# Banded attention and two gated blocks: softmax weights turned in one VectorE instruction per pair and moved by on-chip DMAs

## The chip, the cores and the metric

The kernel runs on one core of one Trainium2 chip. The metric is the device time of one execution in microseconds, the median of three runs. Engines are named as in the profile: PE is TensorE (matrix products; PEld its weight loads), DVE is VectorE, ACT is ScalarE, POOL is GpSimd, SP is SyncE, whose queue issues the DMAs here.

## What is computed

Eight batches of 576 tokens go through an attention of eight heads of width 64 and two gated blocks of width 512. Each query sees at most 32 keys: itself and the 31 before it in heads 0 to 3, every fourth of the 128 positions up to itself in heads 4 to 7.

```python
def _attn_ref(q, k, v):
    scores = scale * np.matmul(q, k.transpose(0, 1, 3, 2))
    mask_plain = (rel >= 0) & (rel < window)                       # window 32
    mask_dil = (rel >= 0) & (rel < window * dilation) & (rel % dilation == 0)   # dilation 4
    scores = np.where(masks[None, :, :, :], scores, -1000000000.0)
    scores = scores - np.max(scores, axis=-1, keepdims=True)
    attn = np.exp(scores)
    attn = attn / (np.sum(attn, axis=-1, keepdims=True) + 1e-09)
    return np.matmul(attn, v)

def _moe_ref(x, w_val, conv_w, w_out):        # gate: causal convolution over 5 tokens
    gate = 1.0 / (1.0 + np.exp(-gate_pre))
    return (gate * (x @ w_val)) @ w_out

def _moe2_ref(x, w_in, w_spatial, b_spatial, w_out):
    h = np.maximum(x @ w_in, 0.0)             # u and v are its halves
    v_n = (v - mu) / np.sqrt(var + 1e-06)
    v_s = np.einsum('ts,bsd->btd', w_spatial, v_n) + b_spatial[None, :, None]
    return (u * v_s) @ w_out
```

## The kernel before

**Attention.** A batch is worked on in four pairs of heads. The 576 queries of a head form 18 blocks of 32, and a block sees 64 keys in a row (tokens of the dilated heads are ordered by their remainder by four first). The score tile of a pair, s_ps, has 128 partitions and nine slots of 64 keys. Partition quarter 2e + h holds block BLOCK[e][x] of head h in slot x. For batch 0 `a_scores` (L287) makes 36 products, each with 64 rows of keys and queries of one head and 32 query columns. For the other batches (L281) it makes 18 of full height, in which the queries of the two heads stand apart with zeros beside them. PE works on each product of float32 in two passes, so a pair leaves 72 or 36 records in the trace. `a_max` (L300 to L307), `a_exp` (ACT) and `a_sum` (L329 to L333, the last of them on POOL) make the weights e_t, a tile of one buffer.

**Turning the weights.** The product with the values needs keys on partitions. The tile pt holds the weights turned, in a form of 128 partitions (keys) by six groups of three blocks. Its zeros are written once, with batch 0, whose weights PE turns. For the other batches `a_trans` issues 16 DVE transposes per pair (L367), one for each partition quarter, half of the 64 keys and run of slots that goes to one place in pt: eight of 32 by 192 elements, eight of 32 by 96. `a_pv` (L384) multiplies six groups for two heads, 12 products into o_ps, which ACT copies to xt (L389, L391). `a_split` makes xh on ACT and xl = xt − xh on POOL; `a_conv` (L417, L419) makes the gate's convolution with five DVE instructions; `a_tanh` ends it on ACT.

**The gated blocks.** A batch is 37 steps: eight val steps (12 products each from xh, xl and the split weight), five v, eight u, eight sp and eight out. A step's products share one of four PSUM buffers of the pool ps_m. val is emptied by DVE (L459), u by ACT, sp by DVE's vb and ru (L546, L547), then split by ACT (g2h) and POOL (g2l), out by ACT (ob), which SP stores (L560). Products of split weights count three for one: high by high, high by low, low by high.

**What sets the order.** The steps of batch b are events 0 to 36. Attention of batch b + 1 is put among them by a table, pair p at 8 p plus an offset: scores 0, max 1, exp 3, sum 3.6, transposes 9, pv 10, split 11, conv 11.2, tanh 12.5. Pair 3's transposes so stand at 33, among the eight out steps (29 to 36). Batch 0's attention is ordered by hand (PRELUDE), and the making of the weights from float64 is placed in batch 0 by a table (FIRST). A scheduler then orders each engine's instructions by its own estimate of when they can run, so the order on an engine is not that of the code.

**Buffers.** s_ps and o_ps have one buffer each; qk, vv, xt and most short-lived tiles have two. The loads of the pair two further on are issued in `a_scores` and `a_pv`, as soon as the old tile has been read.

Of the kernel before, what the change touches and what calls it, by code (L numbers as in the profile page):

```python
# [8 lines left out]
F32 = mybir.dt.float32  # L9
# [20 lines left out]
QZ = KEYS + 2 * S  # the same with the queries of the two heads set apart by zeros  # L30

# Queries come in 18 blocks of 32. Partition half e, slot x of a score tile holds block BLOCK[e][x] of
# both heads. Block 3 j + i sees keys 32 i to 32 i + 63 of group j. RUNS are slots with one i each.
# [7 lines left out]
# Upper words of the float64 that float32's range begins and ends with, read as float32.  # L41
# [3 lines left out]
# What is issued before the first batch's matrix products, in order, and what goes in between them,  # L45
# with its place among them.
# [105 lines left out]
def attention_gated_mlp_kernel(  # L152
    ctx: ExitStack,
    tc: tile.TileContext,
    qk0: bass.AP,
# [23 lines left out]
    pt = const.tile([128, NJ, 3, 2, QB], F32, name="pt")  # L179
# [11 lines left out]
    def weight(name):  # L191
        # A weight whose memory serves something else until the weight is made.
        if name not in held:
            held[name] = wts.tile(LATE[name], F32R, tag=name, name=name)
        return held[name]
# [5 lines left out]
    def split(raw, hi, lo):  # L201
        # raw = hi + lo exactly, where hi has the bits that one pass carries.
        nc.scalar.copy(out=hi, in_=raw)  # L203
        nc.gpsimd.tensor_tensor(out=lo, in0=raw, in1=_f(hi), op=ALU.subtract)  # L204
# [17 lines left out]
    # ---- attention: one batch and one pair of heads at a time  # L222
# [14 lines left out]
    def load_qk(b, p):  # L237
        b, p = b + p // NP, p % NP
        if b == B:
            return  # L240
        if b == 0 and p >= 2:
            t = early_tile(p)
        else:
            t = rot.tile([128, QZ], F32, tag="qk", name="qk_t")
        if b == 0:
            nc.sync.dma_start(out=t[:, 0:QC], in_=qk0[p])
        else:
            nc.sync.dma_start(out=t, in_=qk[b - 1, p])
        qk_t[b, p] = t
# [21 lines left out]
    def a_scores(b, p):  # L271
        t = qk_t.pop((b, p))
        s = ps_s.tile([128, 1024], F32, tag="s", name="s_ps")
        for i in range(2 * NS):
            x, e = divmod(i, 2)
            n = BLOCK[e][x]
            cols = slice(SW * x, SW * x + SW)
            keys = slice(QB * n, QB * n + SW)
            if b:
                q = t[:, KEYS + 64 * i:KEYS + 64 * i + 64]  # L280
                nc.tensor.matmul(s[64 * e:64 * e + 64, cols], q, t[:, keys], start=True, stop=True)  # L281
                continue
            for h in range(2):
                r = slice(64 * h, 64 * h + 64)
                q = t[r, KEYS + QB * n:KEYS + QB * n + QB]
                o = 64 * e + QB * h
                nc.tensor.matmul(s[o:o + QB, cols], q, t[r, keys], start=True, stop=True)  # L287
        if b or p >= 2:
            load_qk(b, p + 2)
        s_t[b, p] = s  # L290
# [44 lines left out]
    def a_trans(b, p):  # L335
        # The weights of the values, with keys on the partitions. TensorE turns the first batch's and
        # writes the zeros as well, which stay; VectorE turns the others'.
        e = e_t.pop((b, p))
        if b == 0:
# [10 lines left out]
            for g in range(3):  # L350
                ps = ps_m.tile([128, 512], F32, tag="m", name="t_ps")
                for i in range(3):
                    nc.tensor.transpose(ps[:, chunk(i)], padded[:, 3 * g + i, :], ident_sb)
                for q in range(2):
                    j, i = divmod(BLOCK[q][3 * g], 3)
                    nc.scalar.copy(
                        out=pt[:, j:j + 3, i],
                        in_=ps[:, 0:384].rearrange("p (j e h q) -> p e j h q", j=3, e=2, h=2)[:, q],
                    )
            return  # L360
        for q, lo, hi in RUNS:
            j, i = divmod(BLOCK[q][lo], 3)
            for h in range(2):
                r = 32 * (2 * q + h)
                for c in range(2):
                    k = 32 * (i + c)
                    nc.vector.transpose(  # L367
                        out=pt[k:k + 32, j:j + hi - lo, i, h], in_=e[r:r + 32, lo:hi, 32 * c:32 * c + 32]
                    )

    def a_pv(b, p):
# [8 lines left out]
        for j in range(NJ):  # L380
            c = 512 * (j // 3) + 96 * (j % 3)
            for h in range(2):
                r = slice(64 * h, 64 * h + 64)
                nc.tensor.matmul(o[r, c:c + 96], u[:, j, r], pt[:, j, :, h], start=True, stop=True)  # L384
# [38 lines left out]
    def a_tanh(b, p):  # L423
        # sigmoid(g) = (1 + tanh(g / 2)) / 2, the half of which goes into w2.
# [4 lines left out]
        (0, a_scores), (1, a_max), (3, a_exp), (3.6, a_sum), (9, a_trans),  # L429
# [6 lines left out]
    # ---- the two gated blocks: one batch, in steps of one accumulation each  # L436

    def mlp_steps(b):
# [29 lines left out]
        def vstep(i):  # L468
# [11 lines left out]
            else:  # L480
                # The last 64 tokens: the two parts of g sit side by side and are added afterwards.
# [18 lines left out]
        def vnorm(i):  # L500
# [7 lines left out]
            if i == 4:  # L508
                # The last 64 tokens a second time, of which the rest stays.
# [58 lines left out]
    # ---- weights: from float64 to float32, the two linear maps in a row made one, and split  # L568
# [25 lines left out]
    def from64(dst, src):  # L594
        # Sign and top bit of the exponent, its low bits and 20 of the mantissa from the upper word
        # (kept inside float32's range), three of the mantissa from the lower word.
# [58 lines left out]
    def fuse(key, e):  # L655
        # w2 = moe_w_out @ moe2_w_in / 2, one chunk of rows and one half of the columns.
# [17 lines left out]
    # ---- everything in order  # L674
# [28 lines left out]
def _layout(q, k, v, moe_w_val, moe_conv_w, moe_w_out, moe2_w_in, moe2_w_spatial, moe2_b_spatial, moe2_w_out):  # L703
# [3 lines left out]
    # The dilated heads see every fourth token: with tokens ordered by their remainder they see a  # L707
    # window like the others.
# [8 lines left out]
    order = np.array(BLOCK).T.reshape(-1)  # L717
    qk0 = np.zeros((NP, 2, D, QC), q.dtype)
    qk = np.zeros((B - 1, NP, 2, D, QZ), q.dtype)
    vv = np.zeros((B, NP, 128, NJ, 2, D), v.dtype)  # L720
    for p in range(NP):
        for hh in range(2):
            h = 2 * p + hh
            qt, kt = qp[:, h].transpose(0, 2, 1), kp[:, h].transpose(0, 2, 1)
            qk0[p, hh, :, 32:KEYS] = kt[0]
            qk0[p, hh, :, KEYS:] = qt[0]
            apart = np.zeros((B - 1, D, 2 * NS, 2, QB), q.dtype)
            apart[:, :, :, hh, :] = qt[1:].reshape(B - 1, D, 2 * NS, QB)[:, :, order]
            qk[:, p, hh, :, 32:KEYS] = kt[1:]
            qk[:, p, hh, :, KEYS:] = apart.reshape(B - 1, D, 2 * S)  # L730
# [8 lines left out]
    def words(w):  # L739
# [17 lines left out]
        ("qk0", qk0.reshape(NP, 128, -1)),  # L757
        ("qk", qk.reshape(B - 1, NP, 128, -1)),
# [32 lines left out]
```

## Time and profile before

| | us |
|---|---|
| median of three runs | 737.53 (736.53, 737.77, 737.53) |
| the profiled execution, as its span | 735.2 |
| left between that span and the median | 2.3 |
| PE busy | 681.2 (93%) |
| DVE busy | 605.4 (82%) |
| POOL, ACT busy | 319.9 (44%), 279.9 (38%) |

The profiled execution is a run of its own; the profile gives its time as the span from the first to the last instruction, and what lies around that span is in the median. The busy shares are means over stages that differ. In the first 180 us the weights are converted, multiplied together and split beside batch 0. Six stretches of 82 us follow, each with the blocks of one batch and the attention of the next. The last batch has no attention beside it. A stretch is delimited here by where val of a batch begins: 504.47 and 586.72 us for one.

### The profile page before, as it was taken

The numbers are of one execution on the slowest core, as the hardware profiler recorded it, in microseconds if no ns is written. First come the engines' busy times: TensorE is split into PE (matmuls) and PEld (weight loads), VectorE is DVE, ScalarE is ACT, GpSimd is POOL, SyncE is SP. The second block draws the span as 40 slices with busy tenths as digits, with TensorE's granted clock in tenths as the row PEclk, the third lists the DMA queues.
The fourth block names the chain that finished last, engine by engine and source line by source line (L and its number), as shares of the span: only waits on it lengthen the run. The fifth ranks groups of instructions, "written<-read, shape, count | busy, mean of one in ns | idle before, by whom it ended". The sixth has DMA issues, their size and how long they took to land.

```text
span 735.2 us, 14508 instructions
## 1 busy us (share of the span) xinstructions
PE 681.2 (93%) x5796; PEld 610.1 (83%) x5796; DVE 605.4 (82%) x1233; ACT 279.9 (38%) x603; POOL 319.9 (44%) x362
## 2 busy tenths in 40 slices
PE   3797999879999899989999899989998999989998
PEld 3455688768899798989899798979898898979898
DVE  5999889999699789996899789997899789984430
ACT  4664435224343324334343334333343334233422
POOL 2527945442644244344544254344534254344421
PEclk9998999989999999999999999999999999999999
DMA  8951023314022221313222221213222220001001
GB/s 345 403 190 49 2 79 120 126 52 136 22 71 72 87 77 53 106 53 112 71 72 81 79 97 48 98 46 112 72 72 80 85 93 22 24 25 42 1 1 64
DMA packets 22179, 63.24 MB, mean 86 GB/s; under 512 B 2528, under 2 KB 11104, under 8 KB 21600
## 3 DMA queue, kind: packets, MB, share of 16 engines
q1 hardware_dynamic: 22112, 62.32, 24.3%
q8 instruction: 45, 0.74, 0.4%
q14 instruction: 22, 0.18, 0.1%
HBM read 52.88 MB, written 9.44 MB: 85 GB/s over the span
## 4 chain that ended last, share of the span: by engine, by line
DVE 46%; PE 38%; issue 8%; ACT 4%; POOL 3%; DMA 1%; SPq 0%; ACTq 0%; DVEq 0%; POOLq 0%
DVE pt L367 14%; PE val_ps L208 12%; PE v_ps L208 8%; DVE tt L419 8%; PE out_ps L208 7%; DVE ru L547 3%; DVE vb L546 3%; PE u_ps L208 3%; PE w_ps L208 3%; PE sp_ps L208 2%; DVE v_t L502 2%; DVE st L490 2%; PE o_ps L384 2%; DVE sm L329 2%; PE s_ps L281 2%
## 5 line engine op out<-in xcount | busy, mean ns | idle before, releaser
L367 DVE STREAM_TRANSPOSE pt<-e_t 32x96 f32<-32x96 f32 (+1 forms) x448 | 143.1, 319 | 9.2 <-PE o_ps L384 1.4
L419 DVE SCALAR_TENSOR_TENSOR tt<-xt,cw,tt 128x576 f32<-128x576 f32 x128 | 134.1, 1049 | 2.2
L208 PE MATMUL sp_ps<-wsp_h,vh 128*128 128x288 f32 x320 | 94.9, 301 | 5.9 <-DVE vb L546 4.9
L204 POOL TENSOR_TENSOR g2l<-ru,g2h 128x288 fp32r<-128x288 f32 x64 | 58.8, 931 | 88.2 <-ACT g2h L203 83.7
L208 PE MATMUL out_ps<-g2h,wout_h 128*128 128x288 f32 x256 | 80.2, 314 | 18.3 <-DVE vb L546 11.8
L208 PE MATMUL sp_ps<-wsp_l,vh 128*128 128x288 f32 x320 | 93.5, 298 | 3.0 <-POOL wsp_l L204 3.0
L208 PE MATMUL out_ps<-g2l,wout_h 128*128 128x288 f32 x256 | 77.6, 304 | 0.0
L208 PE MATMUL u_ps<-gh,w_h 128*128 128x288 f32 x256 | 77.1, 301 | 0.0
L208 PE MATMUL sp_ps<-wsp_h,vl 128*128 128x288 f32 x256 | 76.0, 297 | 0.0
L208 PE MATMUL out_ps<-g2h,wout_l 128*128 128x288 f32 x256 | 75.9, 300 | 0.0
L208 PE MATMUL u_ps<-gh,w_l 128*128 128x288 f32 x256 | 75.5, 295 | 0.0
L208 PE MATMUL u_ps<-gl,w_h 128*128 128x288 f32 x256 | 75.5, 295 | 0.0
L204 POOL TENSOR_TENSOR gl<-tt,gh 128x288 fp32r<-128x288 f32 x64 | 53.3, 839 | 47.3 <-ACT gh L203 47.1
L208 PEld LDWEIGHTS out_ps<-g2h,wout_h 128*128 128x128 f32 x256 | 49.1, 192 | 24.7 <-DVE vb L546 15.3
L514 POOL TENSOR_TENSOR vl<-v_t,vh 128x512 fp32r<-128x512 f32 x32 | 42.0, 1315 | 57.6 <-ACT vh L506 57.6
L208 PEld LDWEIGHTS sp_ps<-wsp_h,vh 128*128 128x128 f32 x320 | 60.5, 189 | 7.8 <-DVE vb L546 5.7
L208 PE MATMUL val_ps<-xh,wval_h 128*128 128x288 f32 x224 | 66.6, 298 | 0.2
L208 PE MATMUL val_ps<-xl,wval_h 128*128 128x288 f32 x224 | 66.4, 296 | 0.0
L208 PE MATMUL val_ps<-xh,wval_l 128*128 128x288 f32 x224 | 66.0, 295 | 0.0
L426 ACT ACTIVATE tt<-tt 128x576 f32<-128x576 f32 x32 | 22.0, 686 | 109.5 <-DVE tt L419 105.5
L208 PEld LDWEIGHTS sp_ps<-wsp_l,vh 128*128 128x128 f32 x320 | 60.6, 190 | 3.1 <-POOL wsp_l L204 3.1
L208 PE MATMUL v_ps<-w_h,gh 128*128 128x512 f32 x160 | 60.9, 405 | 0.0
(129 smaller groups left out, 1688.3 us busy)
## 6 DMA issues: line engine op xcount, KB each, us to landing
qk_t<-in_qk SPq DMA_DIRECT2D x28, 880.0 KB, 4.5
vv_t<-in_vv SPq DMA_DIRECT2D x30, 384.0 KB, 3.1
out<-ob SPq DMA_DIRECT2D x64, 144.0 KB, 1.8
raw<-in_w_in SPq DMA_DIRECT2D x4, 1024.0 KB, 9.1
raw<-in_w_mid_t SPq DMA_DIRECT2D x2, 1024.0 KB, 9.7
raw<-in_w_val SPq DMA_DIRECT2D x2, 1024.0 KB, 13.5
raw<-in_w_out SPq DMA_DIRECT2D x4, 512.0 KB, 4.5
sp_raw<-in_w_sp_t SPq DMA_DIRECT2D x5, 288.0 KB, 2.9
```

Source lines behind the costliest of these rows:

```text
L204: nc.gpsimd.tensor_tensor(out=lo, in0=raw, in1=_f(hi), op=ALU.subtract)
L208: nc.tensor.matmul(o, a, r, start=(i == 0), stop=(i == len(pairs) - 1))
L281: nc.tensor.matmul(s[64 * e:64 * e + 64, cols], q, t[:, keys], start=True, stop=True)
L329: nc.vector.tensor_reduce(out=sm[:, :, 0], in_=e, axis=AX.X, op=ALU.add)
L367: nc.vector.transpose(out=pt[k:k + 32, j:j + hi - lo, i, h], in_=e[r:r + 32, lo:hi, 32 * c:32 * c + 32])
L384: nc.tensor.matmul(o[r, c:c + 96], u[:, j, r], pt[:, j, :, h], start=True, stop=True)
L419: nc.vector.scalar_tensor_tensor(out=t, in0=xt[:, k:k + S], scalar=cw[:, p, k:k + 1], in1=t, op0=ALU.mult, op1=ALU.add)
L426: nc.scalar.activation(out=t, in_=t, func=ACTF.Tanh, scale=0.5)
L490: nc.vector.bn_stats(out=st, in_=v)
L514: nc.gpsimd.tensor_tensor(out=low["v"][:, i], in0=v, in1=_f(h), op=ALU.subtract)
L546: nc.vector.tensor_tensor(out=tmp, in0=ps[:, 0:HS], in1=bb[:, h], op=ALU.add)
L547: nc.vector.tensor_tensor(out=r, in0=tmp, in1=r, op=ALU.mult)
```

## The change

`a_trans` for batches 1 to 7 turns the whole weight tile with one DVE transpose, 32 by 32 inside each partition quarter, into a new tile et of one buffer. Sixteen DMAs from SP's queue then carry its pieces to pt: eight of 32 partitions by 192 elements, eight by 96, in runs of 768 and 384 bytes. pt is laid out anew so that each piece is one run per partition. The offset of `a_trans` in the table goes from 9 to 6. `a_scores` uses the products of batch 0 for all batches, 36 per pair with 32 query columns each; the queries are loaded without zeros, 592 KB per pair for 880, and the separate input qk0 goes. In all, 448 transposes become 28, with 448 more DMAs of together 8.3 MB, and the loads shrink by about 8 MB.

```diff
-    pt = const.tile([128, NJ, 3, 2, QB], F32, name="pt")
+    pt = const.tile([128, 3, 2, NJ, QB], F32, name="pt")
...
-            t = rot.tile([128, QZ], F32, tag="qk", name="qk_t")
-        if b == 0:
-            nc.sync.dma_start(out=t[:, 0:QC], in_=qk0[p])
-        else:
-            nc.sync.dma_start(out=t, in_=qk[b - 1, p])
+            t = rot.tile([128, QC], F32, tag="qk", name="qk_t")
+        nc.sync.dma_start(out=t[:, 0:QC], in_=qk[b, p])
...
-            if b:
-                q = t[:, KEYS + 64 * i:KEYS + 64 * i + 64]
-                nc.tensor.matmul(s[64 * e:64 * e + 64, cols], q, t[:, keys], start=True, stop=True)
-                continue
             for h in range(2):
                 r = slice(64 * h, 64 * h + 64)
                 q = t[r, KEYS + QB * n:KEYS + QB * n + QB]
...
+        t = act.tile([128, 2, NS, QB], F32, tag="et", name="et")
+        nc.vector.transpose(
+            out=t.rearrange("p c x q -> p x c q"), in_=e.rearrange("p x (c k) -> p x c k", c=2)
+        )
         for q, lo, hi in RUNS:
             j, i = divmod(BLOCK[q][lo], 3)
-            for h in range(2):
-                r = 32 * (2 * q + h)
-                for c in range(2):
-                    k = 32 * (i + c)
-                    nc.vector.transpose(
-                        out=pt[k:k + 32, j:j + hi - lo, i, h], in_=e[r:r + 32, lo:hi, 32 * c:32 * c + 32]
-                    )
+            for c in range(2):
+                k = 32 * (i + c)
+                for h in range(2):
+                    r = 64 * q + 32 * h
+                    nc.sync.dma_start(out=pt[k:k + 32, i, h, j:j + hi - lo], in_=t[r:r + 32, c, lo:hi])
...
-                nc.tensor.matmul(o[r, c:c + 96], u[:, j, r], pt[:, j, :, h], start=True, stop=True)
+                nc.tensor.matmul(o[r, c:c + 96], u[:, j, r], pt[:, :, h, j], start=True, stop=True)
...
-        (0, a_scores), (1, a_max), (3, a_exp), (3.6, a_sum), (9, a_trans),
+        (0, a_scores), (1, a_max), (3, a_exp), (3.6, a_sum), (6, a_trans),
```

The order on DVE in a steady batch, where the sp steps end and the out steps begin. vb and ru empty a sp step, the tt rows are the convolution of pair 2, the transposes those of pair 3. Before:

```order
L417 TENSOR_SCALAR tt<-xt,cw 128x576
L419 SCALAR_TENSOR_TENSOR tt<-xt,cw,tt 128x576
L367 STREAM_TRANSPOSE pt<-e_t 32x6x32 x4
L367 STREAM_TRANSPOSE pt<-e_t 32x3x32
L546 TENSOR_TENSOR vb<-sp_ps,bb 128x288
L367 STREAM_TRANSPOSE pt<-e_t 32x3x32 x4
L419 SCALAR_TENSOR_TENSOR tt<-xt,cw,tt 128x576
L367 STREAM_TRANSPOSE pt<-e_t 32x3x32 x3
L367 STREAM_TRANSPOSE pt<-e_t 32x6x32 x4
L546 TENSOR_TENSOR vb<-sp_ps,bb 128x288
L547 TENSOR_TENSOR ru<-vb,ru 128x288
L419 SCALAR_TENSOR_TENSOR tt<-xt,cw,tt 128x576
```

After, lines moved by a few (L354 is the transpose, L540 vb, L541 ru, L413 the convolution):

```order
L322 RECIPROCAL sm<-sm 128x9
L354 STREAM_TRANSPOSE et<-e_t 128x9x2x32
L411 TENSOR_SCALAR tt<-xt,cw 128x576
L540 TENSOR_TENSOR vb<-sp_ps,bb 128x288
L413 SCALAR_TENSOR_TENSOR tt<-xt,cw,tt 128x576
L541 TENSOR_TENSOR ru<-vb,ru 128x288
L540 TENSOR_TENSOR vb<-sp_ps,bb 128x288
L413 SCALAR_TENSOR_TENSOR tt<-xt,cw,tt 128x576
L541 TENSOR_TENSOR ru<-vb,ru 128x288
L413 SCALAR_TENSOR_TENSOR tt<-xt,cw,tt 128x576 x2
```

The sixteen transposes, which stood in three pieces around two vb, are one instruction ahead of them.

The order on PE, where the out steps of a batch end. o_ps rows are the pv products of pair 3. Before, among the last out steps:

```order
L208 MATMUL out_ps<-g2h,wout_h 128x288
L384 MATMUL o_ps<-pt,vv_t 64x96 x2
L208 MATMUL out_ps<-g2l,wout_h 128x288
L208 MATMUL out_ps<-g2h,wout_l 128x288
L208 MATMUL out_ps<-g2l,wout_h 128x288
L208 MATMUL out_ps<-g2h,wout_l 128x288
L384 MATMUL o_ps<-pt,vv_t 64x96 x9
L208 MATMUL out_ps<-g2h,wout_h 128x288
```

After, with the last out product first; s_ps is pair 0 of the batch after:

```order
L206 MATMUL out_ps<-g2l,wout_h 128x288
L206 MATMUL out_ps<-g2h,wout_l 128x288
L278 MATMUL s_ps<-qk_t 32x64 x5
L378 MATMUL o_ps<-pt,vv_t 64x96
L278 MATMUL s_ps<-qk_t 32x64 x3
L378 MATMUL o_ps<-pt,vv_t 64x96 x11
L206 MATMUL val_ps<-xh,wval_h 128x288
```

The pv products of pair 3 have gone from among the out products to behind the last of them, with val of the next batch right after.

The val products that follow them, each tile with its number: 6009 and 6065 are the first two val steps, xh_5981 is the part of x that pair 3's pv makes.

```order
L206 MATMUL val_ps_6009<-xh_5797,wval_h_798 128x288
L206 MATMUL val_ps_6009<-xl_5314,wval_h_798 128x288
L206 MATMUL val_ps_6009<-xh_5797,wval_l_799 128x288
L278 MATMUL s_ps_6025<-qk_t_5475 32x64 x28
L206 MATMUL val_ps_6065<-xh_5313,wval_h_798 128x288
L206 MATMUL val_ps_6065<-xl_5314,wval_h_798 128x288
L206 MATMUL val_ps_6065<-xh_5313,wval_l_799 128x288
L206 MATMUL val_ps_6065<-xh_5542,wval_h_798 128x288
L206 MATMUL val_ps_6009<-xh_5981,wval_h_798 128x288
```

The product that needs the newest part of x stands behind the scores and four products of the second val step.

The order on SP in a steady batch, around the stores of the out steps (L560). Before:

```order
L560 DMA out<-ob 128x288 x6
L259 DMA vv_t<-in_vv 128x768
L560 DMA out<-ob 128x288 x2
L248 DMA qk_t<-in_qk 128x1760 x2
L259 DMA vv_t<-in_vv 128x768 x2
L560 DMA out<-ob 128x288 x16
```

After (L554 the stores, L363 the DMAs to pt, L243 and L254 the loads):

```order
L254 DMA vv_t<-in_vv 128x768
L363 DMA pt<-et 32x192 x4
L363 DMA pt<-et 32x96
L554 DMA out<-ob 128x288
L363 DMA pt<-et 32x96 x2
L554 DMA out<-ob 128x288
L363 DMA pt<-et 32x96 x5
L363 DMA pt<-et 32x192 x4
L554 DMA out<-ob 128x288 x4
L254 DMA vv_t<-in_vv 128x768
L554 DMA out<-ob 128x288 x2
L243 DMA qk_t<-in_qk 128x1184
```

Between two stores there are now up to nine of the sixteen DMAs to pt of pair 3.

## Rows read from the trace of the kernel before

**Rows 1.** The page's busy shares, and its chain of waits by engine.
```profile
PE 681.2 (93%) x5796; PEld 610.1 (83%) x5796; DVE 605.4 (82%) x1233; ACT 279.9 (38%) x603; POOL 319.9 (44%) x362
...
DVE 46%; PE 38%; issue 8%; ACT 4%; POOL 3%; DMA 1%; SPq 0%; ACTq 0%; DVEq 0%; POOLq 0%
```

**Rows 2.** Windows, one period: us, busy (x instructions) by engine, PEclk, DMA share, GB/s.
```profile
504.47:586.72 82.25, 79.17 (x698) 72.69 (x697) 72.08 (x156) 29.73 (x59) 34.74 (x41) 1.00 0.24 79
```

**Rows 3.** Waits of the whole run: engine, line, waited for: us in total, times, longest.
```profile
PE out_ps L208 <- DVE vb L546: 11.8, 12, 1.3
PE sp_ps L208 <- DVE vb L546: 4.9, 6, 0.9
...
PE out_ps L208 <- ACT wout_h L203: 4.6, 1, 4.6
...
PE sp_ps L208 <- POOL wsp_l L204: 3.0, 1, 3.0
...
PE out_ps L208 <- ACT g2h L203: 1.8, 6, 0.3
```

**Rows 4.** PE's timeline: start us, us, instruction, count [idle before <-releaser].
```profile
556.49 0.40 PE L208 MATMUL sp_ps<-wsp_h,vh 128*128 128x288 f32 x1 [0.80 <-DVE vb L546]
...
569.97 0.40 PE L208 MATMUL out_ps<-g2h,wout_h 128*128 128x288 f32 x1 [1.31 <-DVE vb L546]
...
583.43 0.30 PE L208 MATMUL val_ps<-xh,wval_h 128*128 128x288 f32 x1
583.56 0.29 PE L208 MATMUL val_ps<-xl,wval_h 128*128 128x288 f32 x1
```

**Rows 5.** DVE's timeline at the same boundary of the same batch.
```profile
567.65 1.78 DVE L367 STREAM_TRANSPOSE pt<-e_t 32x192 f32<-32x192 f32 x5
569.46 0.46 DVE L546 TENSOR_TENSOR vb<-sp_ps,bb 128x288 f32<-128x288 f32 x1
...
587.32 0.75 DVE L300 TENSOR_TENSOR e_t<-s_ps,mask_sb 128x576 f32<-128x576 f32 x1
```

**Rows 6.** Groups by line and shape: count | busy, mean ns of one | idle before.
```profile
L419 DVE SCALAR_TENSOR_TENSOR tt<-xt,cw,tt 128x576 f32<-128x576 f32 x128 | 134.1, 1049 | 2.2
...
L367 DVE STREAM_TRANSPOSE pt<-e_t 32x192 f32<-32x192 f32 x224 | 82.6, 369 | 4.4 <-POOL e_t L333 1.3
...
L367 DVE STREAM_TRANSPOSE pt<-e_t 32x96 f32<-32x96 f32 x224 | 60.5, 270 | 4.8 <-PE o_ps L384 1.4
```

**Rows 7.** PE's timeline: scores of the first batch, then of a later one.
```profile
11.00 2.14 PE L287 MATMUL s_ps<-qk_t 64*32 64x64 f32 x72 [3.31 <-DVE mx L302]
...
18.62 0.90 PE L353 MATMUL t_ps<-ident_sb,boot 128*128 128x128 f32 x3 [1.69 <-POOL boot L344]
...
26.63 1.21 PE L287 MATMUL s_ps<-qkv 64*32 64x64 f32 x72
27.77 1.20 PE L353 MATMUL t_ps<-ident_sb,boot 128*128 128x128 f32 x9
...
600.78 1.27 PE L281 MATMUL s_ps<-qk_t 128*64 128x64 f32 x36
```

**Rows 8.** SyncE's queue at the start, two issues one behind the other.
```profile
1.18 0.42 SPq L263 DMA_DIRECT2D mask_sb<-in_masks  x1
1.64 0.42 SPq L246 DMA_DIRECT2D qk_t<-in_qk  x1
```

**Rows 9.** The page's DMA issues: count, size, median us from issue to landing.
```profile
out<-ob SPq DMA_DIRECT2D x64, 144.0 KB, 1.8
```

**Rows 10.** A semaphore wait on PE's weight queue, min/median/max ns, in 540 to 543 us.
```profile
L384 PEldq EVENT_SEMAPHORE  x1: 51/51/51, 540.3 to 540.3; - x1
```

**Rows 11.** Groups by shape: the copy of xt, and the low part of x.
```profile
L204 POOL TENSOR_TENSOR xl<-xt,xh 128x576 fp32r<-128x576 f32 x28 | 46.0, 1643 | 27.9 <-ACT xh L203 27.9
...
L391 ACT COPY xt<-o_ps 128x576 f32<-128x576 f32 x16 | 19.3, 1204 | 1.1 <-PE o_ps L384 1.1
```

**Rows 12.** Windows, 5 us in batch 0 (columns of rows 2).
```profile
155.00:160.00 5.00, 4.21 (x15) 3.57 (x15) 4.80 (x14) 0.62 (x1) 1.28 (x1) 0.54 0.02 5
```

More of the change, by code (lines that the diff above doesn't have):

```diff
@@ L29 @@
 QC = KEYS + S
-QZ = KEYS + 2 * S
 BLOCK = [
@@ L154, in attention_gated_mlp_kernel @@
     tc: tile.TileContext,
-    qk0: bass.AP,
     qk: bass.AP,
@@ L356, in a_trans @@
                     nc.scalar.copy(
-                        out=pt[:, j:j + 3, i],
-                        in_=ps[:, 0:384].rearrange("p (j e h q) -> p e j h q", j=3, e=2, h=2)[:, q],
+                        out=pt[:, i, :, j:j + 3],
+                        in_=ps[:, 0:384].rearrange("p (j e h q) -> p e h j q", j=3, e=2, h=2)[:, q],
                     )
             return
+        t = act.tile([128, 2, NS, QB], F32, tag="et", name="et")
+        nc.vector.transpose(
+            out=t.rearrange("p c x q -> p x c q"), in_=e.rearrange("p x (c k) -> p x c k", c=2)
+        )
         for q, lo, hi in RUNS:
             j, i = divmod(BLOCK[q][lo], 3)
-            for h in range(2):
-                r = 32 * (2 * q + h)
-                for c in range(2):
-                    k = 32 * (i + c)
-                    nc.vector.transpose(
-                        out=pt[k:k + 32, j:j + hi - lo, i, h], in_=e[r:r + 32, lo:hi, 32 * c:32 * c + 32]
-                    )
+            for c in range(2):
[3 more added lines that the diff above has]
+                    nc.sync.dma_start(out=pt[k:k + 32, i, h, j:j + hi - lo], in_=t[r:r + 32, c, lo:hi])
     def a_pv(b, p):
@@ L716, in _layout @@
     qp, kp, vp = heads(q), heads(k), heads(v)
-    order = np.array(BLOCK).T.reshape(-1)
-    qk0 = np.zeros((NP, 2, D, QC), q.dtype)
-    qk = np.zeros((B - 1, NP, 2, D, QZ), q.dtype)
+    qk = np.zeros((B, NP, 2, D, QC), q.dtype)
     vv = np.zeros((B, NP, 128, NJ, 2, D), v.dtype)
@@ L724, in _layout @@
             qt, kt = qp[:, h].transpose(0, 2, 1), kp[:, h].transpose(0, 2, 1)
[L725 to L730, printed above, removed]
+            qk[:, p, hh, :, 32:KEYS] = kt
+            qk[:, p, hh, :, KEYS:] = qt
             for j in range(NJ):
@@ L756, in _layout @@
     return [
-        ("qk0", qk0.reshape(NP, 128, -1)),
-        ("qk", qk.reshape(B - 1, NP, 128, -1)),
+        ("qk", qk.reshape(B, NP, 128, -1)),
         ("vv", vv.reshape(B, NP, 128, -1)),
```

## The prediction

> **What bounds the kernel now.** I read the page's busy shares first. PE is busy for 681.2 us of the 735.2 us span, DVE for 605.4; the chain of waits gives DVE 46% and PE 38% [rows 1]. The chain tempts one to count every DVE microsecond saved as won; the stretches show that most of it cannot be. I cut the span where val of a batch begins, so that one stretch holds one batch of the MLP and the attention of the next: the periods are alike, 82.25 us, with PE busy for 79.17 and DVE for 72.08 [rows 2]. So in the steady batches PE sets the pace, and DVE can give back at most the 82.25 − 79.17 = 3.1 us per period in which PE is idle. Next, whom PE waits for: out_ps on vb 11.8 us, sp_ps on vb 4.9, out_ps on g2h 1.8, together 18.5 us, in counts of twelve, six and six [rows 3]; 18.5 / 6 = 3.1, so this is all of PE's idle time, once per steady period. PE's timeline shows the place: 0.80 us at a sp step, 1.31 where out begins [rows 4]. DVE's timeline shows the cause: vb, which empties the PSUM that PE waits for, starts at 569.46, straight behind five transposes that take 1.78 us together [rows 5]. What counts is therefore how much of 3.1 us per period goes, not how much work leaves DVE.
>
> **The transposes.** Sixteen of them per pair go, eight of 369 ns and eight of 270 ns [rows 6]: 448 × 319 = 143.1 us. From the two sizes, one element per partition costs (369 − 270) / 96 = 1.03 ns, and 171 ns is fixed. The new one turns 576 elements per partition: 576 × 1.03 + 171 = 0.77 us if the quarters go side by side, 4 × 576 × 1.03 + 171 = 2.54 us if they go one behind the other. Only one-quarter instructions stand in the trace; I take 0.77, since other DVE instructions work on 128 partitions at such a rate (1.82 ns per element for a two-input step of 1049 ns on 576 [rows 6], no four times that). DVE saves 143.1 − 28 × 0.77 = 121.6 us, 17 us per period (at 2.54: 72 us, 10 per period). Either is more than three times PE's idle 3.1 us, so DVE, at 72.1 − 17 = 55 of 82, has room for vb at once. In the new order one transpose and one 0.5 us step stand ahead of the first vb at the boundary and a conv step and one ru between it and the next, where five transposes and a conv step stood ahead and eleven and another between them. I count the 18.5 us as gone: **−18.5**.
>
> **The 16 DMAs per pair** take the turned weights to pt on SP's queue, 448 in all; the bytes, 8.3 MB, about equal those the smaller query load saves. SP issues follow each other 0.46 us apart [rows 8]; a 144 KB store lands 1.8 us after its issue [rows 9], and issues overlap, since that is four times the spacing. The last of 16 then lands 0.77 + 16 × 0.46 + 1.8 = 9.9 us after the transpose begins, two stores of out between them make it 10.9. PE wants pt late: were the transpose of pair 3 no earlier than its first one is now, 567.65 [rows 5], the last piece would land at 578.6, and PE reaches the end of out at 583.43 now [rows 4], 580.3 without its 3.1 us of waits. It is moved from offset 9 to 6 on top of that. So hidden, by 1.7 us at the least for pair 3, more for the others: 0. What it costs without that cover is rival B. The pv products now wait for about 14 DMA semaphores a pair; such a wait on PE's queue takes 51 ns, 2 us ahead of the product [rows 10]: 28 × 14 × 0.051 = 20 us if nothing covers them, 0 if all are queued ahead. I take **+1.5**, near the row, which lies wholly in PE's shadow.
>
> Here the Trainium skill speaks against the change: "DMA: Bandwidth & Descriptors", section "Rules for kernel authors", wants many small transfers made one, since under 64 KB one pays mostly overhead; these are of 24 and 12 KB. The fixed 2.0 us of its section on the anatomy of one DMA agree with the 1.8 us here; paid one after another they would be 32 us per pair, an estimate from that page. The spacing in rows 8 says that issues don't wait for landings, and I go by it.
>
> **The scores** take 72 matmul records of 64 rows by 32 columns a pair for 36 of full height. The first batch already has both: 72 in 1.21 us against 36 in 1.27 [rows 7], 28 × 0.06 = **−1.7**. The early ones at 2.14 us run where other products are slow too (three t_ps in 0.90 us there, nine in 1.20 later), hence a slower PE; no clock is on record there.
>
> **The order** breaks PE's stream of products by attention more often, 95 times for 87, some 0.2 us each (a product takes 0.40 us after a break and 0.30 in a row [rows 4], once for the attention's and once for the MLP's; an estimate): **+1.6**. Pair 3's pv stands behind all of out; four val steps go between it and what it makes. Behind the copy of xt (1.2 us on ACT [rows 11]) DVE now has five conv steps (four of 1.05 us [rows 6] and a shorter one, some 4.7) and, among them, three steps of the next pair of 0.75 [rows 5] before it empties val: 1.2 + 4.7 + 2.3, some 9 us with the hops between engines, against 48 products at the 0.135 us between starts [rows 4], 6.5, and 1.9 for the scores and breaks, 8.4, until PE wants a fifth buffer of the four. I take 0.5 × 6 = **+3.0**, between 0 and 2 × 6.
>
> **Batch 0 and its neighbours.** DVE is nearly full there, PE runs at a clock of 0.54 of full in one stretch (4.21 us busy of 5) [rows 12], and PE waits for wout_h 4.6 and wsp_l 3.0 us [rows 3]. With less in front of it on DVE the chain that makes wout_h comes earlier, while in the new order POOL makes the first wout_l ahead of the last wsp_l, which holds sp up by as much as 3.8. I take **−2**, between −14 and +6.
>
> **The sum**: 735.2 − 18.5 + 1.5 − 1.7 + 1.6 + 3.0 − 2.0 = 719.1 of span. Around the span lie 2.3 us (737.5 − 735.2), so 721.4; I say **721.5**. Against the median, 737.53, that is −2.2%.
>
> **Rivals.**
>
> A, batch 0 freed too. If the 17 us per batch that DVE saves come off the stretch in which DVE is full, −14 for −2 there, plus nothing lost at val: 721.5 − 12 − 3 = 706. For it: DVE is at 4.80 of 5 there [rows 12]. Against: the weights' work on ACT and POOL and the low clock stay.
>
> B, slower than before: the 16 DMAs per pair can't be issued fast enough. With x us for each, the last piece of pair 3 lands 0.77 + 18x + 1.8 behind the transpose at 567.65; it meets 580.3 at x = 0.56. With the earlier transpose, some 2 us more, it meets it at 0.67. Beyond that every further 0.1 costs 1.8 us a pair, and at x = 0.8 it costs about 2.4 us for pair 3 and 1.8 for the rest, 25 us in six periods, beside some in batch 0: 721.5 + 28 = 750. (With no overlap at all, 16 × 1.8 = 29 us a pair would set the pace, 115 us a period; the issues of rows 8 rule that out for loads.) It makes the change a loss where it eats the 2.7 us per period that the sum gains, from x of about 0.75 on. For it: no transfer from on-chip memory to itself stands in the trace, its spacing is unknown, and each waits for the semaphore lane of the one eight before. Against: 0.46 for several kinds of load [rows 8].
>
> C, the scores at the early pace: 72 in 2.14 us for 1.27, 28 × 0.87 = 24: 745 at the most, 741 with some hidden in DVE waits. For it: [rows 7], 11.00. Against: 26.63. The Trainium skill, "TensorEngine Tiling (Array Packing)", section "Instruction Overhead", has about 60 cycles for each matmul however small; at 2.4 GHz that is 25 ns, an estimate from that page, 1.8 us for 72. Row 26.63 shows 1.21 / 72 = 17 ns and disagrees.
>
> D, the gain is lost to a new wait: val's first products need xh (ACT) and xl (1.64 us on POOL [rows 11]), which follow the pv that stands last. If the four val steps don't cover that and the fifth's buffer comes 2 us later, 2.2 us a period: 721.5 + 13 = 735.
>
> **How the numbers follow.** Forecast 54%, A 13%, B 16%, C 5%, D 12%. What this kernel's measurement tells from no change is about 0.2%, 736.05 to 739.0. The forecast and A are faster; D lies at the edge, half of it faster and most of the rest the same; B and C are slower. Faster 0.70, same 0.08, slower 0.22. The range: down to A and a little beyond it, 703; up past C and D, with the semaphores' upper bound 721.5 + 20 inside it, 743. B at its price of 750 is left out.
>
> **What would show it.** Right: periods of 79.5 to 80 us, PE waits on vb near zero, one transpose of 0.7 to 0.9 us a pair, 72 scores in 1.2 us, DVE near 484 busy. Wrong: pv products released by DMAs into pt (B), val_ps by ACT's xh, POOL's xl or DVE's tt for over 1 us a period (D), scores of 2 us (C), a transpose of 2.5 us, batch 0 shorter by 10 us (A) or longer by 5.

## The result, and the profile after

The changed kernel takes 720.58 us (median of 719.46 to 720.89), the kernel before 737.65 in the same comparison: a ratio of 0.977, 95% interval 0.9756 to 0.9783. The forecast was 721.5 us, −2.2%. The profiled execution spans 718.6 us, where the working gave 719.1.

The page's busy shares and its chain of waits by engine, after (before: [rows 1]):

```profile
PE 679.6 (95%) x6804; PEld 609.0 (85%) x6804; DVE 494.8 (69%) x813; ACT 281.1 (39%) x603; POOL 315.0 (44%) x362
...
PE 73%; DVE 13%; ACT 3%; DMA 3%; issue 3%; POOL 3%; SPq 2%; DVEq 0%; ACTq 0%; POOLq 0%
```

DVE is rid of 110.6 us, PE's work has hardly changed, and the span fell by 16.6. The chain, which was 46% DVE, is now 73% PE. Windows of batch 0 (from val to val) and of batch 1, columns as in [rows 2]. Before:

```profile
52.92:174.36 121.44, 106.21 (x773) 89.38 (x771) 112.51 (x197) 49.14 (x91) 69.84 (x61) 0.93 0.24 81
174.36:254.47 80.11, 76.93 (x624) 70.72 (x625) 64.78 (x149) 29.89 (x60) 35.58 (x41) 1.00 0.18 60
```

After, and behind them the period that answers to [rows 2]:

```profile
54.65:175.89 121.24, 104.57 (x1016) 87.85 (x1013) 99.55 (x144) 50.87 (x94) 72.58 (x64) 0.94 0.25 80
175.89:251.03 75.14, 75.14 (x652) 69.95 (x650) 44.04 (x77) 27.01 (x56) 30.83 (x37) 1.00 0.21 65
490.18:569.82 79.64, 79.40 (x841) 72.99 (x840) 56.39 (x95) 29.66 (x59) 33.96 (x41) 1.00 0.27 85
```

The period is 79.64 us for 82.25, and PE is busy for 79.40 of it: only 0.24 us are left. (The stretch of [rows 2] is cut 3.3 us behind the first val product of its batch, which stands at 501.18; it is a whole period all the same.) Over the six stretches of batches 1 to 6, PE's idle time, length less busy time, went from 18.6 us to 1.2. Batch 0 is as long as before (121.24 for 121.44). Batch 1 is shorter by 5.0 us, more than its idle time of 3.2, because fewer of the attention's products fall behind the cut between the two (652 records in all, where a steady period after has 841; before it was 624 for 698). Batches 0 and 1 together take 196.4 us for 201.6.

Whom PE waits for, whole run (before: [rows 3]):

```profile
PE sp_ps L206 <- ACT wsp_h L201: 6.9, 1, 6.9
...
PE val_ps L206 <- DVE tt L453: 4.8, 6, 3.4
...
PE out_ps L206 <- DVE vb L540: 0.8, 2, 0.5
```

The waits for vb went from 16.7 us to 0.8. The new one for wsp_h, 6.9 us, stands in batch 0. The one for val's tt is 3.4 us once, in batch 0, and 0.24 in a period. PE's timeline where a batch ends (as [rows 4], the last line there), then the one wait of that period:

```profile
567.80 0.41 PE L278 MATMUL s_ps<-qk_t 64*32 64x64 f32 x10
568.14 0.38 PE L378 MATMUL o_ps<-pt,vv_t 128*64 128x96 f32 x2
568.45 0.31 PE L278 MATMUL s_ps<-qk_t 64*32 64x64 f32 x6
568.69 1.20 PE L378 MATMUL o_ps<-pt,vv_t 128*64 128x96 f32 x22
569.82 0.40 PE L206 MATMUL val_ps<-xh,wval_h 128*128 128x288 f32 x1
```

```profile
498.69 0.40 PE L206 MATMUL val_ps<-xh,wval_h 128*128 128x288 f32 x1 [0.24 <-DVE tt L453]
```

The pv products of pair 3 run without a wait. Their way there: the transpose on DVE's timeline, its group, and the DMAs of the same pair on SP's timeline (start, us, count):

```profile
552.09 0.78 DVE L354 STREAM_TRANSPOSE et<-e_t 128x576 f32<-128x576 f32 x1 [1.26 <-POOL e_t L324]
```

```profile
L354 DVE STREAM_TRANSPOSE et<-e_t 128x576 f32<-128x576 f32 x28 | 21.6, 772 | 26.0 <-POOL e_t L324 18.5 <-DMA pt<-et 4.5 <-POOL gl L202 1.7
```

```profile
552.89 3.33 SPq L363 DMA_DIRECT2D pt<-et  x5
557.38 0.35 SPq L554 DMA_DIRECT2D out<-ob  x1
557.78 1.14 SPq L363 DMA_DIRECT2D pt<-et  x2
559.45 0.35 SPq L554 DMA_DIRECT2D out<-ob  x1
559.85 5.57 SPq L363 DMA_DIRECT2D pt<-et  x9
```

The nine last of these DMAs, by line (ns min/median/max, first and last start), and their landing:

```profile
L363 SPq DMA_DIRECT2D pt<-et x9: 507/589/590, 559.8 to 564.8; - x9
...
DMA to landing us min/median/max: 1.7/1.8/1.8
```

An issue to pt holds SP's queue for 0.59 us and they follow each other 0.63 us apart (5.0 us for eight steps), not 0.46 as the loads of [rows 8] do; a landing takes 1.8 us as supposed. The last piece of pair 3 is in pt at 564.8 + 1.8 = 566.6 us, and PE wants it at 568.14: 1.5 us to spare. Worked out in the same way from the DMA records of the other pairs, the spare time in the steady batches is 0.2 to 1.5 us for pairs 1, 2 and 3 and 2.3 to 3.5 for pair 0. So the DMAs are hidden, by little.

### The profile page after: what moved, and what is told of

The parts are those of the page before. It is cut to its first block, busy times and chain, and to the rows that moved or that the text cites. A ratio compares the mean times of both kernels' runs of the same rounds, so it can differ in the third digit from the quotient of the medians.

```text
span 718.6 us, 16806 instructions
## 1 busy us (share of the span) xinstructions
PE 679.6 (95%) x6804; PEld 609.0 (85%) x6804; DVE 494.8 (69%) x813; ACT 281.1 (39%) x603; POOL 315.0 (44%) x362
## 4 chain that ended last, share of the span: by engine, by line
PE 73%; DVE 13%; ACT 3%; DMA 3%; issue 3%; POOL 3%; SPq 2%; DVEq 0%; ACTq 0%; POOLq 0%
PE sp_ps L206 15%; PE v_ps L206 14%; PE u_ps L206 13%; PE out_ps L206 11%; PE val_ps L206 9%; DVE tt L413 6%; PE o_ps L378 5%; PE s_ps L278 3%; PE w_ps L206 3%; SPq L363 2%; DMA out<-ob 1%; POOL boot L336 1%; ACT xt L385 1%; DVE tt L411 1%; DMA raw<-in_w_mid_t 1%
## 5 line engine op out<-in xcount | busy, mean ns | idle before, releaser
L413 DVE SCALAR_TENSOR_TENSOR tt<-xt,cw,tt 128x576 f32<-128x576 f32 x128 | 137.6, 1076 | 1.5
L202 POOL TENSOR_TENSOR g2l<-ru,g2h 128x288 fp32r<-128x288 f32 x64 | 56.7, 892 | 80.8 <-ACT g2h L201 80.8
L202 POOL TENSOR_TENSOR xl<-xt,xh 128x576 fp32r<-128x576 f32 x28 | 44.6, 1594 | 91.2 <-ACT xh L201 91.2
L206 PE MATMUL out_ps<-g2h,wout_h 128*128 128x288 f32 x256 | 76.1, 298 | 2.0 <-DVE vb L540 0.8
L206 PE MATMUL out_ps<-g2l,wout_h 128*128 128x288 f32 x256 | 75.5, 295 | 0.0
L411 DVE TENSOR_SCALAR tt<-xt,cw 128x576 f32<-128x576 f32 x32 | 26.5, 829 | 68.1 <-ACT xt L385 66.2
L206 PE MATMUL val_ps<-xh,wval_l 128*128 128x288 f32 x224 | 65.5, 295 | 0.0
L206 PE MATMUL v_ps<-w_l,gh 128*128 128x512 f32 x160 | 61.9, 401 | 0.0
L201 ACT CAST g2h<-ru 128x288 fp32r<-128x288 f32 x64 | 27.7, 433 | 87.5 <-DVE ru L541 86.8
```

Source lines behind the costliest of these rows:

```text
L206: nc.tensor.matmul(o, a, r, start=(i == 0), stop=(i == len(pairs) - 1))
L411: nc.vector.tensor_scalar(out=t, in0=xt[:, 0:S], scalar1=cw[:, p, 0:1], scalar2=None, op0=ALU.mult)
L413: nc.vector.scalar_tensor_tensor(out=t, in0=xt[:, k:k + S], scalar=cw[:, p, k:k + 1], in1=t, op0=ALU.mult, op1=ALU.add)
```

## The experiments

All times are medians, with the kernel before run beside each (737.2 to 737.5 us). The start of a run up to the first val varies by itself: 52.6 to 54.9 us in the traces, for code that is nearly the same up to there. So a difference of 1 or 2 us says nothing where a steady period does not show it too.

**The scores undone (x_padded).** The changed kernel, with the queries of the two heads apart and zeros between them again.

```diff
+            if b:
+                q = t[:, KEYS + 64 * i:KEYS + 64 * i + 64]
+                nc.tensor.matmul(s[64 * e:64 * e + 64, cols], q, t[:, keys], start=True, stop=True)
+                continue
...
```

> The changed kernel with the padded scores of the kernel before put back (18 products of full height per pair, 880 KB loads). Theory: the scores are nearly neutral, 1.199 us per pair for 1.140 in the trace of the changed kernel, 28 x 0.06 = 1.7 us, so 722.3 us against its 720.6 (720.6 to 724). Rival (the unpadded scores carry the gain, or cost much): over 726, or under 715.

717.65 us, ratio to before 0.9733 (0.9711 to 0.9754). Undoing the unpadded scores makes the kernel faster by 2.7 us, by the two ratios, instead of slower by 1.7. The gain is not theirs. A steady period shows it, at 79.01 us for 79.64, and shows that it is PE's own work, 79.01 us for 79.40:

```profile
486.75:565.76 79.01, 79.01 (x699) 73.30 (x697) 53.75 (x95) 30.43 (x59) 34.23 (x41) 1.00 0.30 94
```

**The scores alone (x_scores).** The kernel before with the unpadded scores and nothing else.

> The kernel before with the unpadded scores alone; transposes and their place as before. Theory: 737.6 - 1.7 = 735.9 (734 to 738), PE's waits for vb and g2h stay near 18 us. Rival (the scores carry the gain): 725 or less.

746.24 us, ratio 1.0121 (1.01 to 1.0142): slower by 9, which neither theory said. Windows, batch 1 and a steady period:

```profile
174.09:261.12 87.03, 79.28 (x770) 72.86 (x769) 69.70 (x151) 29.46 (x59) 36.80 (x41) 0.98 0.15 50
510.30:592.91 82.61, 79.13 (x843) 72.47 (x841) 72.27 (x155) 29.85 (x59) 35.30 (x42) 1.00 0.20 67
```

Batch 1 takes 87.03 us where it took 80.11 before, 4.6 of the 6.9 us more in idle time of PE; a steady period takes 82.61 for 82.25, with the same PE work (79.13 for 79.17). In batch 1, DVE's timeline, then PE's:

```profile
179.94 4.92 DVE L359 STREAM_TRANSPOSE pt<-e_t 32x192 f32<-32x192 f32 x15
184.88 0.82 DVE L451 SCALAR_TENSOR_TENSOR tt<-tt,val_ps 128x288 f32<-128x288 f32 x2
```

```profile
185.39 0.61 PE L207 MATMUL val_ps<-xh,wval_h 128*128 128x288 f32 x1 [4.03 <-DVE tt L451]
```

The scheduler, given other products, put fifteen transposes in a row ahead of the step that empties val, and PE waited for it. The cost is one of order: 36 instructions for 18 shift its plan, and the plan moves the time by more than the products do. With the sixteen transposes in place PE also goes on waiting for vb, for rather longer than the theory's 18 us:

```profile
PE out_ps L207 <- DVE vb L538: 14.3, 14, 2.2
PE sp_ps L207 <- DVE vb L538: 8.3, 7, 1.6
```

**DVE's time put back (x_dve6).** The changed kernel with six idle transposes per pair, 4.6 us, that read et and hold nothing else.

```diff
+        x = act.tile([128, 2, NS, QB], F32, tag="ex", name="ex")
+        for _ in range(6):
+            nc.vector.transpose(out=x.rearrange("p c x q -> p x c q"), in_=t.rearrange("p c x q -> p x c q"))
```

> The changed kernel with six more DVE transposes per pair from et into a tile that nothing reads: 4.6 us per pair, so that DVE spends as long on turning as before (5.4 us), while e_t is let go at once and the DMAs do not wait for them. Theory (the 18.5 us were DVE being late): PE waits for vb or val's tt come back, most of 18 us: 732 to 742. Rival (the new order alone removed the waits): 720 to 726.

747.25 us, ratio 1.0143 (1.0121 to 1.0165): the whole gain goes and 10 us more. But PE does not wait where the theory said. Its waits, whole run:

```profile
PE o_ps L381 <- DMA pt<-et: 12.6, 5, 5.5
...
PE out_ps L206 <- DVE vb L543: 2.1, 1, 2.1
```

A late DVE now shows as late DMAs: the transpose of pair 3 starts 64 to 73 us behind the first val product of its period, in batches 2 to 5, where it stood at 62 in the changed kernel; ten microseconds of DMAs follow, and pv has no time to spare. The waits for vb do not return, though DVE works as much in a period as before the change (74.21 us of 86.48 here, 72.08 of 82.25 in [rows 2]):

```profile
423.31:509.79 86.48, 82.06 (x903) 75.13 (x898) 74.21 (x122) 30.90 (x61) 34.75 (x41) 0.98 0.28 80
```

The scheduler set the extra transposes one at a time among the steps that empty sp, where the sixteen had stood in blocks ahead of vb:

```profile
563.07 0.77 DVE L366 STREAM_TRANSPOSE ex<-et 128x576 f32<-128x576 f32 x1
563.76 0.42 DVE L543 TENSOR_TENSOR vb<-sp_ps,bb 128x288 f32<-128x288 f32 x1
564.10 0.43 DVE L544 TENSOR_TENSOR ru<-vb,ru 128x288 f32<-128x288 f32 x1
564.46 0.77 DVE L366 STREAM_TRANSPOSE ex<-et 128x576 f32<-128x576 f32 x1
```

So it is shown that the changed kernel cannot spare this time of DVE, and refuted that it would come back as waits for vb. In these runs the waits follow what stands ahead of vb more than how much DVE has to do in all; how much of the gain is due to each is not shown, since no run has the old order with the shorter work.

**The same, coarser.** Twelve idle transposes of e_t behind those of pairs 2 and 3 (p >= 2; x_late), or of pairs 0 and 1 (p < 2; x_early).

```diff
+        if p >= 2:
+            x = act.tile([128, 2, NS, QB], F32, tag="ex", name="ex")
+            for _ in range(12):
+                nc.vector.transpose(
+                    out=x.rearrange("p c x q -> p x c q"), in_=e.rearrange("p x (c k) -> p x c k", c=2)
+                )
```

> The changed kernel with DVE work added that nothing uses: twelve more transposes of 0.77 us behind those of pairs 2 and 3, 18.5 us per batch, about what the change took from DVE, where the sp and out steps are. Theory (place decides): vb is late again, PE waits 3 to 6 us per period, 720.6 + 18 to 36 = 738 to 757. Rival (a busy DVE of 75 in 80 us is no matter while PE is the bound): 720 to 724.

> The same twelve more transposes behind those of pairs 0 and 1, beside val, v and u, where DVE has room and little that PE waits for. Theory (place decides, not the amount): 720 to 727, under half of the loss with the late ones. Rival (DVE's total decides): as much as with the late ones, 738 or more.

770.98 and 760.58 us, ratios 1.046 (1.0443 to 1.0477) and 1.0323 (1.0296 to 1.035). The early one costs four fifths of what the late one does (40 us over the changed kernel, for 50), and the theory that its place would be free is refuted. So is the theory of the late one: it lies above its 738 to 757, and PE waits for vb for 2.5 us in the whole run. Both hold e_t, which has one buffer, for 9 us, and so hold up the attention of the next pair. In the late one pair 3's transpose starts 83 us behind val and PE stands idle for some 5 us ahead of that pair's pv; in the early one PE's wait is for the DMAs again:

```profile
PE o_ps L384 <- DMA pt<-et: 18.5, 7, 5.7
```

These two do not tell load from place, since they also delay the chain of the attention; the one above was made for that reason.

**More DMAs.** The same bytes in 24 DMAs per pair (x_24), then in 20 (x_20), then 20 with a second buffer for et (x_20e2). The edit of the first:

```diff
-                    nc.sync.dma_start(out=pt[k:k + 32, i, h, j:j + hi - lo], in_=t[r:r + 32, c, lo:hi])
+                    for y in range(lo, hi, 3):
+                        z = j + y - lo
+                        nc.sync.dma_start(out=pt[k:k + 32, i, h, z:z + 3], in_=t[r:r + 32, c, y:y + 3])
```

> The changed kernel with each of the eight smaller sources of 96 and the eight of 192 elements moved in pieces of 96, so 24 DMAs per pair for 16, the same bytes. Theory (the DMAs are hidden, but by a margin of only 0.2 to 1.5 us as the landings and the pv products of the changed kernel's trace stand, at 0.635 us an issue): eight more issues are 5.1 us, 3.6 to 5 us over the margin, of which pair 3's stands ahead of val: 720.6 + 6 x 4 = 745 (730 to 755), with PE waits of o_ps for the DMAs. Rival (the spare time is several us, as an issue of 0.46 us would leave): 720 to 727.

766.22 us, ratio 1.0393 (1.0371 to 1.0414): 45.6 us for eight issues more per pair, above the theory's 730 to 755, and rival B of the prediction in kind. PE's timeline at the end of a batch, then one whole period and two windows around that end, which closes the period behind it:

```profile
602.72 0.35 PE L380 MATMUL o_ps<-pt,vv_t 128*64 128x96 f32 x2 [2.78 <-DMA pt<-et]
603.86 2.18 PE L380 MATMUL o_ps<-pt,vv_t 128*64 128x96 f32 x22 [0.80 <-DMA pt<-et]
607.31 0.61 PE L206 MATMUL val_ps<-xh,wval_h 128*128 128x288 f32 x1 [1.26 <-ACT ob L555]
```

```profile
433.51:519.72 86.21, 81.62 (x842) 75.08 (x841) 56.83 (x96) 30.42 (x60) 35.61 (x41) 0.96 0.26 75
...
598.56:602.94 4.38, 1.43 (x74) 1.24 (x74) 2.77 (x6) 0.68 (x1) 0.52 (x1) 1.00 0.08 17
602.94:607.32 4.38, 2.32 (x25) 1.90 (x23) 2.29 (x3) 0.46 (x2) 0.63 (x1) 0.55 0.40 116
```

The period is 86.21 us, 6.6 more. PE's idle time in it, 4.6 us, is about the 4 that the theory gave; the rest is PE's own work, 81.62 us for 79.40, at a granted clock of 0.96 for 1.00. Behind the wait at the end of a batch the clock is 0.55, near the lower of its two levels (1.2 of 2.4 GHz).

> The changed kernel with four of the sixteen DMAs of a pair split, 20 for 16, the same bytes. Theory 1 (a ring: et and pt have one buffer each, so a pair's DMAs wait for the landing and the pv of the pair before; a turn of the ring takes n x 0.7 + 4.6 us, four turns are 63 us of the 79.6 us period at 16 and 86 at 24, where 86.4 was measured; at 20 they are 74): 720 to 726, no wait yet. Theory 2 (each issue beyond the margin of about 1 us costs its time once per batch, linear in the number): 24 cost 45 us, so 20 cost about half, 735 to 745.

730.64 us, ratio 0.9916 (0.9893 to 0.9938): 10 us, between the two theories. Theory 1 is refuted, for there is a wait; theory 2 as well, for four cost 10 us and eight 45.6. The cost bends upward from somewhere above 16. Where PE waits now, and ACT's wait for the stores of out in this kernel (37.0 us in the changed one):

```profile
PE val_ps L206 <- ACT ob L555: 9.2, 10, 1.9
...
PE o_ps L380 <- DMA pt<-et: 5.6, 5, 2.0
```

```profile
ACT ob L555 <- DMA out<-ob: 40.1, 16, 8.9
```

> The kernel with 20 DMAs per pair, with two buffers for et in place of one, so that a transpose need not wait until the DMAs of the pair before have read it. If the single et is the link that binds with 20 DMAs: 720 to 725, most of the 10 us gone. If pt (still one tile, which the DMAs of the next pair may write only when pv has read it) or SP's queue binds: 727 to 733, no change against 730.6.

733.75 us, ratio 0.9934 (0.9904 to 0.9964): no change. DVE's wait to write et falls from 8.5 us to 1.3 in the two traces, and the time stays, so the single et is not the link. What is left is pt, which has one tile, and SP's queue, where the stores of out stand among the DMAs to pt and keep ob from being written. The 9.2 us above point at the queue, the 5.6 at the late pieces themselves; which of the two links binds at 20 was not told apart.

**Half of the DMAs on ACT's queue (x_act).**

```diff
-                    nc.sync.dma_start(out=pt[k:k + 32, i, h, j:j + hi - lo], in_=t[r:r + 32, c, lo:hi])
+                    (nc.scalar if h else nc.sync).dma_start(out=pt[k:k + 32, i, h, j:j + hi - lo], in_=t[r:r + 32, c, lo:hi])
```

> The changed kernel with half of the DMAs (head 1 of each pair) issued from ACT's queue, so that eight stand on each of two queues. Theory (the landings are hidden already): no gain from landing some 5 us earlier; ACT pays about 0.6 us for each, 19 us per period on an engine that is busy for 30 of 80, so 719 to 726. Rival (PE waits for the DMAs in a way that the waits do not show): 716 or less.

726.02 us, ratio 0.9852 (0.9835 to 0.9868): 5.4 us slower than the changed kernel, at the upper end of what the theory gave. In the steady batches the last piece of pairs 2 and 3 now lands some 3 to 4 us ahead of pv (that of pair 1 no earlier than before), and nothing is won: with 16 issues they are hidden on SP's queue already. PE is idle for no longer than in the changed kernel (38.9 us of the span for 39.1). The loss is in its own work, 684.3 us for 679.6, which attention breaks up more often: PE goes from one to the other 25 to 34 times in a steady period for 23.

**The place in the table (x_off9).** The changed kernel with a_trans at 9 again.

> The changed kernel with the transposes' place in the table back at 9. Theory: the transposes start when POOL's weights are ready, in both; the scheduler's order comes out much the same in the steady batches, 718 to 724. Rival (the earlier place carries the gain): over 727.

720.88 us, ratio 0.9772 (0.9746 to 0.9799): the same as at 6 in the total, but not stretch by stretch. With 9, batches 0 and 1 take 188.6 us for 196.4, and what follows takes 474.6 for 467.6, its periods 79.9 to 80.6 (a few of the attention's products lie across that cut). The theory's reason does not hold either: pair 3's transpose stands 65.5 us behind val in the steady batches, 3.6 later than with 6, and waits there for its turn and not for POOL (with 6 it waits 1.3 us for POOL, part of the 18.5 in its group above). Its pv has moved along: it stands some 16 us behind the transpose with either place.

**Batch 0.** PE's new wait of 6.9 us there is for wsp_h. ACT's timeline in the changed kernel:

```profile
124.89 0.67 ACT L201 CAST wsp_h<-sp_raw 128x576 fp32r<-128x576 f32 x1 [1.59 <-DMA sp_raw<-in_w_sp_t]
131.23 0.62 ACT L201 CAST wout_h<-wo_f 128x512 fp32r<-128x512 f32 x1 [5.67 <-DVE wo_f L601]
131.76 0.67 ACT L201 CAST wsp_h<-sp_raw 128x576 fp32r<-128x576 f32 x1
```

The last wsp_h stands on ACT behind a wout_h that waits 5.67 us for DVE. So in the table FIRST the loads and splits of the spatial weight went ahead of w_out's (its first steps at 15.93 and 20.655 stayed; v_sp1):

```diff
-    (16.881, ("load_sp", 3)),
...
+    (10.91, ('split_sp', 2)),
+    (10.92, ('split_sp', 0)),
+    (10.93, ('load_sp', 3)),
+    (10.94, ('load_sp', 4)),
...
```

> The changed kernel with the loads and splits of the spatial weight ahead of w_out's first loads in batch 0's table. Theory: the 6.9 us that PE waits for wsp_h there go, some of it to a wait for wout: 714 to 718, the steady periods unchanged. Rival (batch 0 is bound by DVE or the clock): 719 to 723.

715.66 us, ratio 0.9705 (0.9687 to 0.9723). The wait for wsp_h is gone from the trace, one of 4.6 us for wout_h has come, and the steady period is 79.65 us, as before this edit.

In a last version w_out's loads and conversions are earlier too (the first load at 13.5, the first conversion at 17.0), and the padded scores are back (v_padsp2).

> The changed kernel with the padded scores put back and, in batch 0's table, the loads and splits of both the spatial weight and w_out earlier. Theory: the two gains add, 720.6 - 2.9 for the scores - 5 for the spatial weight, and the 4.6 us of waiting for wout_h that was left go in part: 709 to 714. Rival (the scores' 2.9 us came from the same batch-0 stretch): 714 to 718.

711.04 us, ratio 0.9644 (0.9626 to 0.9662). The two gains add, with some 2 us beyond them that may be w_out's or chance, and this version beats both kernels: 1.3% below the changed one. A steady period of it, in which PE is never idle:

```profile
482.78:561.78 79.00, 79.00 (x698) 73.29 (x696) 53.75 (x95) 30.45 (x59) 34.20 (x41) 1.00 0.31 95
```

## Why the prediction held, and where its steps were off

The time and the main mechanism were right. PE set the pace, and DVE's saving was worth only PE's idle time: of 110.6 us taken from DVE, 16.6 came off the span. Of the 18.5 us of waits for vb and g2h, 0.8 are left. The gain comes with the new transposes and their DMAs: without the new scores it stays (x_padded), the new scores alone do not bring it (x_scores), and the place in the table does not change the total (x_off9).

For vb the forecast gave two reasons, that DVE has room and that fewer instructions stand ahead of it. The runs speak for the second: with DVE's time put back (x_dve6) the gain is gone, but through late DMAs, and PE waits for vb for 2.1 us only.

That the sum came within 1 us is luck. PE's idle time in the six stretches of batches 1 to 6 fell by 17.4 us, where the forecast had 18.5 less 3.0 for val, 15.5. PE's own work, with the semaphore waits counted to it, was to grow by 1.4 and fell by 1.7. The idle time elsewhere, in the start, batch 0 and the last batch, was to shrink by 2.0 and grew by 2.5. The three errors, −1.9, −3.1 and +4.5, cancel. Term by term:

- **The DMAs** were counted at 0.46 us an issue, from loads; to pt they take 0.63. By the step's own bound (transpose at 567.65, PE at 580.3, 12.65 us later) 0.77 + 18 × 0.63 + 1.8 = 13.9 us would have been late. They are hidden because pv stands farther behind the transpose: 552.09 is 16 us ahead of the pv at 568.14. The forecast gave "some 2 us more" for this, from the place in the table; it was over 3, and x_off9 has the same 16 us without that place. The conclusion was right with little to spare, and rival B, placed at 0.67 to 0.75 us an issue, was nearer than its 16%: 20 DMAs per pair already cost 10 us and 24 cost 45.6.
- **The semaphores** were +1.5, from 14 waits a pair. The trace has about six a pair on PE's weight queue, 51 ns each in the median, and no wait of PE ahead of a pv product.
- **The scores** were a term of −1.7. Each set is shorter by some 0.06 us, as forecast (72 in 1.14 us to the next product [rows 7], 36 in 1.20), and rival C did not come. The early 2.14 us, 30 ns a record, were probably a low clock: the same scores take 1.50 us for 46, 33 ns each, where the granted clock is 0.52 (last section), and 17 at full clock [rows 7]; no clock is on record at 11.00. But in the whole kernel they cost 2.7 us. A term worked out from one group's duration left out that the scheduler plans anew, and that PE's other products take longer in the new order.
- **The breaks** were +1.6. In the steady period above PE's work is 79.40 us for 79.17; what of this is breaks was not told apart.
- **val's wait** was forecast at 0.5 us a period and is 0.24.
- **Batch 0** was −2 and is −0.2, beside 1.7 us in the start that runs differ by anyway. The forecast named the chains. The wait for wout_h went from 4.6 to 0.4 us, as it said; the wout step ahead of the last wsp, put at up to 3.8 us, cost 3.9, from 3.0 in [rows 3] to 6.9, on ACT, where the forecast had POOL. The two cancel. Rival A, −14 there, did not come, though x_off9, v_sp1 and v_padsp2 show that 5 us and more were there for an edit of the table.

One sign was missed. DVE was to be near 484 us busy and is at 494.8: the transposes fell from 143.1 to 21.6 us, as forecast, and DVE's other instructions take 11 us longer.

The Trainium skill, "DMA: Bandwidth & Descriptors", section "Rules for kernel authors", says that transfers under 64 KB pay mostly overhead. The trace agrees: 12 and 24 KB hold SP's queue for 0.59 us alike. What decided was that this cost overlaps, with 1.5 us to spare at pair 3. The 2.0 us that the prediction took from the same page of the Trainium skill, section "Anatomy of one DMA — SWDGE (gpsimd) path", are given there for DMAs issued from GpSimd; these are issued from SP, and land 1.8 us after their issue. The Trainium skill, "TensorEngine Tiling (Array Packing)", section "Instruction Overhead", has about 60 cycles for each matmul, 25 ns at 2.4 GHz as an estimate from that page. [rows 7] disagree, with 17 ns for each record.

## What to carry to other kernels

Read what a faster engine is worth from the idle time of the engine that sets the pace, one period at a time, and not from the work it saves. Look at what stands ahead of the step that is waited for, not only at how busy its engine is. When work moves from an engine to a queue, price the queue by the same kind of transfer, and ask how many more issues it would bear: here 16 are hidden and 20 are not. Where a scheduler sets the order, a small term that rests on one group's duration is not to be trusted even in its sign.

## What the runs showed of the hardware

A wait of PE costs more than the time it lasts. In the run with twelve late extras, windows of 5 us at the end of a batch, with PE idle in the second and at work again in the third:

```profile
600.00:605.00 5.00, 4.75 (x98) 4.27 (x97) 4.79 (x7) 0.00 (x0) 0.00 (x0) 1.00 0.12 28
605.00:610.00 5.00, 0.09 (x1) 0.12 (x2) 4.72 (x7) 0.00 (x0) 0.00 (x0) 0.80 0.12 30
610.00:615.00 5.00, 5.00 (x82) 4.21 (x83) 1.42 (x4) 2.23 (x4) 1.15 (x1) 0.52 0.76 239
615.00:620.00 5.00, 4.95 (x46) 4.12 (x44) 4.63 (x6) 0.90 (x2) 1.90 (x1) 1.00 0.31 99
```

The scores on PE's timeline in the third of them:

```profile
610.39 1.50 PE L278 MATMUL s_ps<-qk_t 64*32 64x64 f32 x46
```

Some 5 us without a product are followed by 5 us at a granted clock of 0.52, near the level of 1.2 GHz, so that about half of that stretch is lost as well. The waits of 0.3 to 1.3 us in the kernel before left its periods at 1.00 [rows 2]. That is why 24 DMAs per pair, with a clock of 0.55 behind their waits, cost more than the waits themselves.

A small transfer from on-chip memory to itself, of 32 partitions with 768 or 384 bytes each, holds SP's queue for 0.59 us in the changed kernel (the median, both sizes alike), where a store of 144 KB in the same trace holds it for 0.35. Both land 1.8 us after their issue.
